# Attention with ALiBi and an MLP on one Trainium2 core: first q and k loaded in FP32 by other queues, the distances of two blocks added on TensorE, and the norm's gain moved into the copies of turned x

## The chip, the cores and the metric

The kernel runs on one core of a Trainium2 chip. The core has five engines that run their own instruction streams in order: TensorE (PE in the profile; PEld is its weight load), VectorE (DVE), ScalarE (ACT), GpSimd (POOL) and SyncE (SP). They wait for one another by semaphores. Transfers are issued by SyncE, ScalarE and GpSimd and run on 16 DMA engines. The metric is device time in microseconds for the whole call, lower is better.

## What is computed

Inputs are `q`, `k`, `v` of 8 batches x 8 heads x 576 tokens x 64, in FP32, and the MLP's gain (512), `w_ch1` (512 x 2048) and `w_ch2` (2048 x 512).

```python
scores = q @ k.T / sqrt(64);  rel = i - j
scores = where((rel >= 0) & (rel < 128), scores - slope[h] * abs(rel), -1e9)   # slope[h] = 2 ** -(h + 1)
attn = softmax(scores);  x = concat_heads(attn @ v)          # (8, 576, 512)
xn = (x - mean(x)) / sqrt(var(x) + 1e-6) * g_ln
out = x + relu(xn @ w_ch1) @ w_ch2
```

Each query sees at most 128 keys: those of its own block of 128 and of the block before.

## The kernel before

**Tiling.** Batches go in pairs; a pair has nine blocks of 128 query rows: two for each of four stretches of 128 tokens (one per batch, so blocks 0 and 1 are tokens 0 to 127 of the two batches and have no block before them, blocks 2 and 3 are tokens 128 to 255), and a ninth for the last 64 tokens of both. Blocks 0 to 7 make four groups of two, all later ones groups of four. Group 0 is blocks 0 and 1, group 1 blocks 2 and 3.

**One block's way.** The raw tokens of q and k are loaded (`load_qk`, L217: by GpSimd, which casts to FP16 on the way), turned on TensorE (`turn`, L323; `turn_first`, L371, for blocks 0 and 1) through PSUM and copied out by VectorE and ScalarE. `attend` (L405) makes scores in PSUM bank pair `ps_sc[0]` or `ps_sc[1]` in turn, and ScalarE takes the exponent. `masks` (L446) multiplies by `m_full`, `m_ends` or `m_tail` on VectorE: tables of exp(-slope x distance), zero outside the window, that `decay` (L145) makes on ScalarE from a table of distances. `values` (L473, in two halves of four heads) or `values_at_once` (L504) multiplies by v with a column of ones beside it, so that the sum of the weights comes along; VectorE takes the reciprocal and writes x with its row sum. `centre` (L535) subtracts the mean. For blocks 0 to 3 it also multiplies by g, spread over all partitions by a matmul with a row of ones (`spread_g`, L301, `g_row`). `turn_x` (L577) turns the block on TensorE and copies it to `xT`.

**The MLP.** `mlp1` (L736) multiplies one group by w1 in 16 units of 128 hidden rows, four matmuls each, with a Relu after each unit on ScalarE, or on VectorE for the units listed in `on_dve`. `mlp2` (L767) multiplies by w2; its result is scaled by the row's 1/std and added to x. Groups 0 and 1 (`FIRST_GROUPS = 2`) are multiplied by w1 itself, which is why their x carries g; later groups use `w1g`, which `gain_w1` (L188) makes on VectorE.

**Order.** The order on each engine is written out by hand: `steps` is a list of lists of calls. The first ones, up to `first`, run before any MLP work; `weave_at` then runs a group's `mlp1` or `mlp2` and, after the units named by its places, takes further steps. A step's instructions enter each engine's stream at that place. `warm(n)` (L294) puts n matmuls of 512 columns, whose result nobody reads, into TensorE's stream. The part up to `first`:

```python
steps = warm_step(11) + [[(turn_first,)]] + warm_step(3)
steps += [scores_step(0), scores_step(1) + masks_of(0) + masks_of(1)] + warm_step(6)
steps += values_steps(0)
steps += [turn_step(2, True, (nc.scalar.copy, nc.scalar.copy))]
steps += values_steps(1) + warm_step(4)
steps += [x_step(0, nc.scalar.copy)] + warm_step(2) + [scores_step(2)]
steps += [masks_of(2, 1) + x_step(1) + scores_step(3), values_steps(2)[0]]
steps += [masks_of(2)]
```

so all scores of blocks 0 to 3 stand before `mlp1(0)`. Loads have an order of their own (`loads`, `place`, `load_until`), all on GpSimd's queue: q and k of blocks 0 and 1, v0, v1, q and k of blocks 2 and 3, v2, v3, four quarters of w1, half of w2, and so on. At most eight of GpSimd's loads are under way: the ninth waits until the first has landed. SyncE loads the distances, an identity matrix and g.

Of the kernel before, what the change touches and what calls it, by code (L numbers as in the profile page):

```python
# [17 lines left out]
P = 128  # L18
# [45 lines left out]
FAR = 60000.0  # L64


def distances():
# [14 lines left out]
    cols = [m[:, evens_first] for m in both] + [*ends, tail]  # L82
    return np.concatenate(cols, axis=1).astype(np.float16)
# [3 lines left out]
def kernel(  # L87
# [41 lines left out]

    iden_dram = nc.inline_tensor(np.eye(P, dtype=np.float16), name="iden16")  # L130
    dist_dram = nc.inline_tensor(distances(), name="distances")
    dist = consts.tile([P, 5 * P], FP16)
    nc.sync.dma_start(out=dist, in_=dist_dram.ap())
    iden = consts.tile([P, P], FP16)
# [4 lines left out]
    nc.sync.dma_start(out=iden, in_=iden_dram.ap())  # L139
# [5 lines left out]
    def decay(m, at):  # L145

        n = m.shape[2]
        for h in range(H):
            nc.scalar.activation(
                out=m[:, h, :],  # L150
                in_=dist[:, at * P : at * P + n],
                func=AF.Exp,
                scale=-(2.0 ** (-8.0 * (h + 1) / H)),
            )

    g_sb = consts.tile([P, NKB], FP32)
    nc.sync.dma_start(out=g_sb, in_=moe_g_ln.rearrange("(kb p) -> p kb", p=P))

    g_line = out_pool.tile([P, DM], FP32, tag="o", name="g_line")[0:1]
    nc.sync.dma_start(out=g_line, in_=moe_g_ln.rearrange("(o d) -> o d", o=1))  # L160
    g_row = out_pool.tile([P, DM], FP32, tag="o", name="g_row")
    one_line = consts.tile([1, P], FP32)
# [15 lines left out]
    ht_all = consts.tile([P, NFB, 4 * P], FP16)  # L178
    w1r = moe_w_ch1.rearrange("(kb p) f -> p kb f", p=P)
# [86 lines left out]
    weights = {3: w1s + w2s[:2], 5: w2s[2:]}  # L266
    loads, place = [], []
    for n, (p, blk) in enumerate(order):
        of_v = [(load_v, p, blk)]
        if n >= V_FIRST:  # L270
            loads += of_v
        if blk % 2 == 0:
# [27 lines left out]

    def spread_g():  # L301

        ps = ps_mm.tile([P, DM], FP32, tag="mm", name="ps_g")
        nc.tensor.matmul(ps, one_line, g_line, start=True, stop=True)
        return ps
# [65 lines left out]
    def turn_first():  # L371

        q, k = queries(0, 0), keys_tile("k", 0, 0)
        ps = [bank(b)[:, 0] for b in range(2)]
        transposed("q", 0, 0, ps)
        for b in range(2):
            nc.vector.tensor_copy(out=q[:, b], in_=ps[b])
        ps_row = spread_g()
        warm(2)
        ps = [bank(b)[:, 0] for b in (0, None)]  # L380
        transposed("k", 0, 0, ps)
        for b, copy in enumerate((nc.scalar.copy, nc.vector.tensor_copy)):
            copy(out=k[:, b].rearrange("p h (c r) -> p r h c", r=2), in_=ps[b])
        nc.vector.tensor_copy(out=g_row, in_=ps_row)
# [19 lines left out]

    def attend(p, blk, keys, mask, tag, hps, sc=None):  # L405
# [15 lines left out]
        ps = banks.rearrange("p j (n t q) -> p j n t q", n=len(hps), t=nk)  # L421
        qt, b = turned["q", p, blk // 2], blk % 2
        for n, hp in enumerate(hps):
            for t, o in enumerate(keys):
                kt = turned["k", p, o // 2][:, o % 2]
                for c, r, queries in seen(p, blk, o, t):
                    cols = slice(c * HALF, (c + 1) * HALF)
                    for j in range(2):
                        rows = slice(j * HALF, (j + 1) * HALF)
                        nc.tensor.matmul(  # L430
                            in_halves(ps[cols, j, n, t, :])[:, r, queries],
                            kt[rows, hp, cols],
                            in_halves(qt[rows, b, hp])[:, r, queries],
                            start=True,
                            stop=True,
                        )
# [7 lines left out]
        unmasked.setdefault((p, blk), []).append((dst, mask[:, heads, :]))  # L444
# [59 lines left out]
    def values_at_once(p, blk):  # L504
# [3 lines left out]
        ps = ps_sc[0].rearrange("p g (h e) -> p (g h) e", h=4)  # L508
# [26 lines left out]
    def centre(p, blk):  # L535
# [3 lines left out]
        if p * NSLOT + blk < BY_DMA:  # L539
# [13 lines left out]
        if p == 0 and blk < FIRST:  # L553
            nc.vector.scalar_tensor_tensor(
                out=xc,
                in0=xs[p, blk],
                scalar=mean,
                in1=g_row,
                op0=ALU.subtract,
                op1=ALU.mult,  # L560
            )
        else:
            nc.vector.tensor_scalar(  # L563
                out=xc, in0=xs[p, blk], scalar1=mean, scalar2=None, op0=ALU.subtract
            )
# [11 lines left out]
    def turn_x(g, at, p, blk, copy):  # L577
# [6 lines left out]
        copy(out=xT[:, :, at * P : (at + 1) * P], in_=ps)  # L584
# [82 lines left out]


    steps = warm_step(11) + [[(turn_first,)]] + warm_step(3)
    steps += [scores_step(0), scores_step(1) + masks_of(0) + masks_of(1)] + warm_step(6)  # L670
    steps += values_steps(0)
    steps += [turn_step(2, True, (nc.scalar.copy, nc.scalar.copy))]
    steps += values_steps(1) + warm_step(4)
    steps += [x_step(0, nc.scalar.copy)] + warm_step(2) + [scores_step(2)]
    steps += [masks_of(2, 1) + x_step(1) + scores_step(3), values_steps(2)[0]]
    steps += [masks_of(2)]
    first = len(steps)

    steps += [values_steps(2)[1] + masks_of(3)]
    steps += [x_step(2, nc.scalar.copy), *values_steps(3), x_step(3, nc.scalar.copy)]  # L680
# [5 lines left out]
    steps += [values_steps(4)[1], scores_step(5) + [(decay, m_ends, 2)]]  # L686
    steps += [x_step(4) + masks_of(5)]
    steps += [values_steps(5)[0], turn_step(6, True), values_steps(5)[1], scores_step(6)]
    steps += [x_step(5) + masks_of(6), scores_step(7) + variance_of(4), values_steps(6)[0]]
# [471 lines left out]
    nc.vector.memset(ones, 1.0)  # L1161
    for vx in vext:
        nc.vector.memset(vx[:, :, D : D + 1], 1.0)
    nc.vector.memset(magic, 0x5F3759DF)
    nc.vector.memset(one_line, 1.0)
    decay(m_full, 0)
    decay(m_tail, 4)
    load_until(place[3])
    engine = mybir.EngineType
    with tc.manual_schedule(engines={engine.PE}):  # L1170
        with tc.manual_schedule(engines={engine.Activation, engine.DVE, engine.SP, engine.Pool}):
            advance_to(first)
            weave_at(mlp1(0, (0, 1)), 2, 7, 8, 9, 13)
# [60 lines left out]
```

## Time and profile before

| | |
|---|---|
| median of 3 runs | 307.45 us (307.02 to 308.31) |
| the profiled execution | 307.49 us, span of the trace 305.7 us |
| TensorE busy | 297.9 us, 97% of the span |
| VectorE, ScalarE, GpSimd busy | 80%, 60%, 37% |
| moved by DMA | 38.03 MB; HBM read 36.90 MB, written 9.44 MB |

Times in the trace count from the start of the span. A line of a timeline gives the start, how long the group of instructions took, engine and source line, output <- inputs, shape, count, and in brackets the idle time before it with what ended it. A line of the table of waits gives who waited for whom: total us, times, the longest.

### The profile page before, as it was taken

To read this page: it belongs to the slowest core of one execution; us is meant where nothing else is said; L and a number is where in the kernel's file an instruction comes from. 1 tells how busy PE (TensorE), PEld (TensorE's weight loads), DVE (VectorE), ACT (ScalarE), POOL (GpSimd) and SP (SyncE) were. 2 spreads that over 40 slices of the span, in tenths; PEclk is the share of its full clock that TensorE was granted. 3 is DMA by queue.
4 is the path that set the end of the run, shared out by engine and by line. 5 is a ranking of instruction groups with operands and counts; after the bars stand their busy time and mean duration, and the time that the engine had idled before them with its cause. 6 is when DMAs were issued, how large, how long until landed. Compare 5 with 4: busy or idle time off the path is not lost.

```text
span 305.7 us, 9273 instructions
## 1 busy us (share of the span) xinstructions
PE 297.9 (97%) x3782; PEld 203.6 (67%) x3782; DVE 245.7 (80%) x651; ACT 182.4 (60%) x329; POOL 111.7 (37%) x152
## 2 busy tenths in 40 slices
PE   8889999999999999999999999999999999999994
PEld 2468755856755578646865686568656865698883
DVE  2689878889986899679867986798799878978993
ACT  7588775767966863675368635853586268505500
POOL 8923659673774372475107250760000000000000
PEclk9999999999999999999999999999999999999999
DMA  9999999999999999999999999997661043005014
GB/s 112 172 206 200 189 158 165 196 131 100 138 120 193 145 132 141 182 182 132 131 172 130 114 131 159 121 154 95 97 130 38 19 102 72 19 19 137 3 34 103
DMA packets 150172, 38.03 MB, mean 124 GB/s; under 512 B 140785, under 2 KB 146033, under 8 KB 150130
## 3 DMA queue, kind: packets, MB, share of 16 engines
q0 software_dynamic: 103744, 18.36, 89.0%
q1 hardware_dynamic: 45906, 18.70, 37.7%
q8 instruction: 29, 0.48, 0.7%
q10 hardware_dynamic: 480, 0.39, 0.5%
q14 instruction: 13, 0.11, 0.1%
HBM read 36.90 MB, written 9.44 MB: 152 GB/s over the span
## 4 chain that ended last, share of the span: by engine, by line
PE 90%; DMA 5%; POOL 2%; ACT 2%; issue 1%; DVE 0%; ACTq 0%; POOLq 0%
PE ps_m L746 36%; PE ps_s L976 25%; PE ps_m L776 9%; PE ps_sc L430 6%; PE ps_sc L512 4%; PE ps_q L1055 4%; PE ps_x L870 3%; DMA q<-q 3%; DMA k<-in_k_dram 2%; PE ps_pv L483 1%; POOL q L223 1%; ACT probs L438 1%; PE ps_tr L317 1%; PE ps_sc L317 1%; POOL vx L258 1%
## 5 line engine op out<-in xcount | busy, mean ns | idle before, releaser
L746 PE MATMUL ps_m<-xT,w1g 128*128 128x512 f16 (+1 forms) x512 | 103.8, 353 | 0.0
L762 ACT ACTIVATE ht_all<-ps_m 128x512 f16<-128x512 f32 (+1 forms) x143 | 71.7, 511 | 26.5 <-PE ps_m L746 24.5
L438 ACT ACTIVATE probs<-ps_sc 128x1024 f16<-128x1024 f32 x56 | 56.5, 1029 | 46.4 <-PE ps_sc L430 46.4
L746 PEld LDWEIGHTS <-w1g 128*128 128x128 f16 x512 | 47.6, 98 | 42.6 <-issue 0.4
L258 POOL DMA_DIRECT2D vx<-in_v_dram x40 | 34.0, 859 | 67.1 <-PE ps_sc L512 38.4
L976 PE MATMUL ps_s<-w,s 128*128 128x256 f16 x384 | 43.8, 273 | 0.0
L976 PEld LDWEIGHTS <-s 128*128 128x128 f16 x384 | 36.7, 98 | 4.7
L449 DVE TENSOR_TENSOR probs<-probs,m 128x1024 f16<-128x1024 f16 x56 | 36.9, 684 | 2.5 <-ACT probs L438 2.5
L976 PE MATMUL ps_s<-w,ht_all 128*128 128x256 f16 x288 | 34.3, 273 | 0.0
L776 PE MATMUL ps_m<-w,ht_all 128*128 128x512 f16 x128 | 31.3, 380 | 0.0
L976 PEld LDWEIGHTS <-ht_all 128*128 128x128 f16 x288 | 27.4, 98 | 5.0
L247 POOL DMA_DIRECT2D q<-in_q_dram x40 | 27.4, 698 | 4.9 <-DMA vx<-in_v_dram 2.9
L997 DVE SCALAR_TENSOR_TENSOR o<-ps_s,rstd,x 128x256 f32<-128x256 f32 x48 | 21.0, 478 | 8.4 <-PE ps_s L976 8.4
L796 DVE TENSOR_TENSOR s<-ht_all 128x1024 f16<-128x1024 f16 (+2 forms) x36 | 20.5, 571 | 7.9 <-ACT ht_all L762 6.7
L430 PE MATMUL ps_sc<-q,k 64*64 64x128 f16 (+1 forms) x1088 | 24.1, 209 | 1.1 <-ACT probs L438 0.7
L430 PEld LDWEIGHTS <-k 64*64 64x64 f16 x1088 | 15.8, 106 | 13.1 <-issue 10.9
L594 ACT ACTIVATE junk<-xc 128x512 f16<-128x512 f16 x28 | 17.6, 628 | 5.7 <-DVE xc L563 5.6
L244 POOL DMA_DIRECT2D k<-in_k_dram x20 | 17.9, 910 | 6.8 <-DMA k<-k 5.3
L521 DVE SCALAR_TENSOR_TENSOR x<-ps_sc,rec 128x512 f16<-128x512 f32 x28 | 19.4, 692 | 1.0
L997 DVE SCALAR_TENSOR_TENSOR o<-ps_s,rstd,o 128x256 f32<-128x256 f32 x36 | 15.7, 478 | 3.4 <-PE ps_s L976 3.1
L776 PEld LDWEIGHTS <-ht_all 128*128 128x128 f16 x128 | 11.1, 98 | 10.8
L512 PEld LDWEIGHTS <-probs 128*128 128x128 f16 x352 | 14.6, 98 | 3.5
(109 smaller groups left out, 381.8 us busy)
## 6 DMA issues: line engine op xcount, KB each, us to landing
out_dram<-o SPq DMA_DIRECT2D x64, 128.0 KB, 2.4
k<-in_k_dram POOLq DMA_DIRECT2D x32, 128.0 KB, 6.9
vx<-in_v_dram POOLq DMA_DIRECT2D x32, 128.0 KB, 8.0
w<-in_moe_w_ch_dram POOLq DMA_DIRECT2D x8, 512.0 KB, 10.9
q<-in_q_dram POOLq DMA_DIRECT2D x48, 64.0 KB, 6.3
q<-in_q_dram POOLq DMA_DIRECT2D x12, 128.0 KB, 5.4
out_dram<-o SPq DMA_DIRECT2D x10, 64.0 KB, 1.9
k<-in_k_dram POOLq DMA_DIRECT2D x8, 64.0 KB, 6.7
```

Of the source, the lines that this page charges most:

```text
L247: nc.gpsimd.dma_start(out=t[half, b], in_=tokens.rearrange("h (c r) d -> r c h d", r=2)[r],)
L258: nc.gpsimd.dma_start(out=vx[p0 : p0 + n, :, 0:D], in_=v[b, :, t0 : t0 + n, :].rearrange("h p d -> p h d"),)
L430: nc.tensor.matmul(in_halves(ps[cols, j, n, t, :])[:, r, queries], kt[rows, hp, cols], in_halves(qt[rows, b, hp])[:, r, queries], start=Tr ...
L438: nc.scalar.activation(out=dst.rearrange("p (n j) q -> p j n q", j=2), in_=ps.rearrange("p j n t q -> p j n (t q)"), func=AF.Exp, scale=in ...
L449: nc.vector.tensor_tensor(out=dst, in0=dst, in1=mask, op=ALU.mult)
L512: nc.tensor.matmul(ps[:, h, 0 : D + 1], pr[:, h, t, :], vext[(p * NSLOT + o) % NV][:, h, :], start=(n == 0), stop=(n == len(terms) - 1),)
L746: nc.tensor.matmul(ps[:, 0:cols], w[:, kb, fb * P : (fb + 1) * P], xT[:, kb, 0:cols], start=(kb == 0), stop=(kb == NKB - 1),)
L762: nc.scalar.activation(out=ht[:, fb, :], in_=ps[:, 0:cols], func=AF.Relu)
L776: nc.tensor.matmul(sums[at], ht[:, fb, at * P : (at + 1) * P], w2[:, fb, :], start=(fb == 0), stop=(fb == NFB - 1),)
L796: nc.vector.tensor_tensor(out=out, in0=a, in1=b, op=op)
L976: nc.tensor.matmul(ps[:, pair, :], lhs[:, fb, at : at + P], rhs[:, fb, :], start=(first and pair == 0 and fb == 0), stop=(fb == half - 1), ...
L997: nc.vector.scalar_tensor_tensor(out=outs[at][:, cols], in0=ps[:, pair], scalar=rstd[:, n : n + 1], in1=(xs[p, blk] if fresh else outs[at] ...
```

## The change

- **First q and k.** The raw tokens of blocks 0 and 1 are no longer loaded by GpSimd with a cast, but in FP32 by SyncE (q) and ScalarE (k), each batch by itself, into parts of the hidden tile `ht_all` that `mlp1` writes later. q stands in partitions 0 to 63, k in 64 to 127. `turn_first` turns them by FP32 matmuls with an FP32 identity, one batch at a time.
- **GpSimd's queue** starts with v0, v1, the first quarter of w1, q and k of blocks 2 and 3, v2, the second quarter, v3, then the rest of w1 and half of w2. The other half of w2 goes one block earlier, and the tables for `m_ends` and `m_tail` follow as a load of their own.
- **Distances on TensorE.** For blocks 0 and 1 VectorE makes eight tables of -slope x distance x 8 (`slopes`), and TensorE writes them into the score banks by a matmul with the identity (`add_distances`); the scores are added on top. Those blocks need no masks. `FAR` falls from 60000 to 16000.
- **g.** `spread_g` and `g_row` are gone; `centre` only subtracts. For groups 0 and 1 `turn_x` multiplies by g in the copy: on VectorE one operation, on ScalarE four.
- **Order.** There are 7 warm matmuls first, not 11. The steps up to `first` hold blocks 0 and 1 alone; the turn, scores and values of blocks 2 and 3 come in `mlp1(0)`, from its unit 3 on. Relus of units 4, 5 and 6 of `mlp1(0)` go to VectorE too. `m_full` is made in three parts, `m_tail` after block 6's scores. Blocks 0 and 1 use `values_at_once`.

```diff
-FAR = 60000.0
+FAR = 16000.0
+ADDED = 2
...
+    def load_first(queue, src, b):
+        rows = slice(0, HALF) if src is q else slice(HALF, P)
+        queue.dma_start(
+            out=first_qk[b][rows],
+            in_=src[b, :, 0:P, :].rearrange("h (c r) d -> c h r d", r=2),
+        )
+    def load_tables():
+        nc.gpsimd.dma_start(out=more_tables, in_=tables_dram[:, 3 * P :])
+    def slopes():
+        for h in range(H):
+            nc.vector.tensor_scalar(
+                out=bias[:, h],
+                in0=first_tables[:, 2 * P :],
+                scalar1=-(2.0 ** (-8.0 * (h + 1) / H)) / inv_sqrt_d,
+                scalar2=None,
+                op0=ALU.mult,
+            )
...
-    weights = {3: w1s + w2s[:2], 5: w2s[2:]}
+    weights = {1: w1s[:1], 2: w1s[1:2], 3: w1s[2:] + w2s[:2], 4: w2s[2:], 5: [(load_tables,)]}
...
+    def turn_first(b, copy):
...
+        for hp in range(HP):
+            for r in range(2):
+                for t, dst in enumerate(ps):
+                    rows = slice(t * HALF, (t + 1) * HALF)
+                    for j in range(2):
+                        cols = slice(j * HALF, (j + 1) * HALF)
+                        nc.tensor.matmul(
+                            dst[cols, r, hp, :],
+                            first_qk[b][rows, 2 * hp + j, r, :],
+                            iden32[rows, rows],
+                            start=True,
+                            stop=True,
+                        )
+        nc.vector.tensor_copy(out=q[:, b], in_=ps[0])
+        copy(out=k[:, b].rearrange("p h (c r) -> p r h c", r=2), in_=ps[1])
...
+    def add_distances(banks):
+        for j in range(2):
+            nc.tensor.matmul(
+                banks[:, j].rearrange("p (n c) -> p n c", n=HP),
+                iden,
+                bias.rearrange("p (n j) c -> p j n c", j=2)[:, j],
+                start=True,
+                stop=False,
+                skip_group_check=True,
+            )
...
-                            start=True,
+                            start=not added,
...
-        if p == 0 and blk < FIRST:
-            nc.vector.scalar_tensor_tensor(
-                out=xc,
-                in0=xs[p, blk],
-                scalar=mean,
-                in1=g_row,
-                op0=ALU.subtract,
-                op1=ALU.mult,
-            )
...
-        copy(out=xT[:, :, at * P : (at + 1) * P], in_=ps)
+        dst = xT[:, :, at * P : (at + 1) * P]
+        if g >= FIRST_GROUPS:
+            copy(out=dst, in_=ps)
+            return
+
+        if copy == nc.vector.tensor_copy:
+            nc.vector.tensor_tensor(
+                out=dst, in0=ps, in1=g_sb.unsqueeze(2).broadcast_to([P, NKB, P]), op=ALU.mult
+            )
+            return
+        for kb in range(NKB):
+            nc.scalar.activation(
+                out=dst[:, kb], in_=ps[:, kb], func=AF.Copy, scale=g_sb[:, kb : kb + 1]
+            )
...
+    (low2, high2), (low3, high3) = ([[(attend, *args)] for args in attends(*order[n])] for n in (2, 3))
+    steps = warm_step(7)
+    steps += [[(slopes,), (nc.vector.tensor_copy, iden32, iden), (decay, m_full, range(3))]]
+    steps += [[(turn_first, 0, nc.scalar.copy)], [(add_distances, ps_sc[0])]]
+    steps += [[(decay, m_full, range(3, 5))]]
+    steps += [[(turn_first, 1, nc.vector.tensor_copy)], [(add_distances, ps_sc[1])]]
+    steps += [scores_step(0), scores_step(1)] + warm_step(3)
+    steps += [[(values_at_once, 0, 0, 0), (centre, 0, 0)]] + warm_step(3)
+    steps += [[(values_at_once, 0, 1, 1)], x_step(0, nc.scalar.copy), [(centre, 0, 1)]] + warm_step(2)
+    steps += [x_step(1)]
     first = len(steps)
+    steps += [[(decay, m_full, range(5, H))] + turn_step(2)] + warm_step(3)
+    steps += [low2, high2 + masks_of(2, 1)] + warm_step(2) + [low3 + masks_of(2)]
+    steps += [values_steps(2)[0], high3 + masks_of(3, 1), values_steps(2)[1]]
+    steps += [values_steps(3)[0], x_step(2), values_steps(3)[1], x_step(3)]
...
+    def start():
+        load_first(nc.sync, q, 0)
+        load_first(nc.scalar, k, 0)
+        nc.sync.dma_start(out=first_tables, in_=tables_dram[:, 0 : 3 * P])
+        load_first(nc.scalar, k, 1)
+        load_first(nc.sync, q, 1)
+        nc.sync.dma_start(out=g_sb, in_=moe_g_ln.rearrange("(kb p) -> p kb", p=P))
+        load_until(place[3])
...
-            weave_at(mlp1(0, (0, 1)), 2, 7, 8, 9, 13)
+            weave_at(mlp1(0, (0, 1, 4, 5, 6)), 3, 3, 3, 3, 3, 3, 4, 5, 6, 7, 8, 9, 11)
```

More of the change, by code (lines that the diff above doesn't have):

```diff
@@ L81, in distances @@
     both = [far(P + query - key), far(query - key)]
-    cols = [m[:, evens_first] for m in both] + [*ends, tail]
+    cols = [np.eye(P), *(m[:, evens_first] for m in both), *ends, tail]
     return np.concatenate(cols, axis=1).astype(np.float16)
@@ L127 @@
     )
[L130 to L134, printed above, removed]
+    tables_dram = nc.inline_tensor(tables(), name="tables").ap()
+    first_tables = consts.tile([P, 3 * P], FP16)
+    more_tables = consts.tile([P, 3 * P], FP16)
+    iden = first_tables[:, 0:P]
+    iden32 = consts.tile([P, P], FP32)
     ps_sc = [
```

93 lines of the change are left out of this document (39 added, 54 removed).

## The prediction

> **What bounds the kernel now.** I read the page first, then the waits of TensorE, then the timelines of TensorE, ScalarE and VectorE over the first 50 us.
>
> ```profile
> PE 90%; DMA 5%; POOL 2%; ACT 2%; issue 1%; DVE 0%; ACTq 0%; POOLq 0%
> ```
> ```profile
> PE ps_warm L299 <- DVE vx L1163: 1.5, 1, 1.5
> PE ps_sc L430 <- ACT probs L438: 0.7, 2, 0.5
> PE ps_sc L317 <- DMA k<-in_k_dram: 0.6, 2, 0.4
> PE ps_tx L583 <- DVE xc L554: 0.3, 1, 0.3
> ```
> The chain that ends last is TensorE. All its waits lie before 19.2 us: asked for the rest of the span, the table of waits shows none. So what counts is when TensorE has done a given amount of useful work; from there the end follows at a fixed distance. The timeline of TensorE gives the marks:
>
> ```profile
> 1.46 4.88 PE L299 MATMUL ps_warm<-ones 128*128 128x512 f16 x11 [1.46 <-DVE vx L1163]
> 6.26 0.44 PE L317 MATMUL ps_sc<-iden,q 64*64 64x64 f16 x32
> 6.64 1.12 PE L304 MATMUL ps_g<-g_line,one_line 1*128 1x512 f32 x2
> 10.07 1.47 PE L299 MATMUL ps_warm<-ones 128*128 128x512 f16 x6
> ...
> 19.16 1.47 PE L746 MATMUL ps_m<-xT,w 128*128 128x256 f16 x12
> ...
> 26.65 8.02 PE L746 MATMUL ps_m<-xT,w 128*128 128x256 f16 x72
> ```
> The 72 are units 14 and 15 of group 0's first product (8 matmuls, 0.11 us each) and the 64 of group 1's. **Mark M**, the first matmul of `mlp1(1)`, is at 26.65 + 0.87 = 27.5 us. By M both kernels have done the same useful work (scores, values and turned x of blocks 0 to 3, all of `mlp1(0)`); behind it TensorE's order is the same. So the change is worth the shift of M, as long as nothing behind it is moved. The difference inside: before, blocks 2 and 3 have their scores done when `mlp1(0)` starts at 19.16; afterwards only blocks 0 and 1 have.
>
> **The change, part by part: the front.** I walk the new order with these rows.
>
> ```profile
> 3.05 2.56 ACT L149 ACTIVATE m<-dist 128x256 f16<-128x256 f16 x8 [1.03 <-DMA dist<-distances]
> 9.97 1.94 ACT L438 ACTIVATE own<-ps_sc 128x1024 f16<-128x1024 f32 x2 [0.52 <-PE ps_sc L430]
> ```
> ```profile
> 9.39 0.67 DVE L384 COPY g_row<-ps_g 128x512 f32<-128x512 f32 x1
> 14.04 0.75 DVE L554 SCALAR_TENSOR_TENSOR xc<-x,mean,g_row 128x512 f16<-128x512 f16 x1
> ...
> 31.27 4.30 DVE L193 TENSOR_SCALAR w1g<-w,g_sb 128x512 f16<-128x512 f16 x13
> ```
> *Tables.* `dist` (160 KB), alone, landed at 3.05. Now q and k of batch 0 (0.52 MB in FP32) share the way with 0.1 MB of tables. The loads of the page's 5 to 10 us wrote 158 GB/s in FP16, so read 316 GB/s; 0.46 MB more is 1.5 us: 4.4 us (ends: 3.05, as `dist`, and 6.0, if q1, k1 and v0 take their part too). Batch 1 lands near 7.
>
> *VectorE before the first turn.* Eight `slopes` and the copy to `iden32` stand before it: nine of 128x128, between 0.08 (a quarter of L193's 0.33) and 0.21 (a 128x1 `mean`); I take 0.14, so 1.3 us. The first turn starts at 5.8.
>
> *FP32 turns.* 32 matmuls of 64 columns per batch. The L304 pair took 1.05 us to the next matmul for 512 columns, so 0.13 us for 64; the FP16 turns ran 32 in 0.28 us, which at 0.027 us each (64 columns at the 0.215 us per 512 of the later warm matmuls) is some 3 side by side. Hence 1.2 us a batch; ends 0.28 (no dearer than FP16) and 4.2 (one after another). The first is at half speed until 6.3 (the first eleven warm matmuls are 0.44 apart, the later ones 0.215): 5.8 to 7.3. `add_distances`, two of 512, 0.44: 7.7. Second turn to 8.9, its distances to 9.3.
>
> *Copies, softmax, values.* An FP32 copy of 512 columns is L384's 0.6 apart. VectorE has q1, k1 from 9.1 to 10.4; scores of block 1 at 10.5, its exponent on ScalarE (0.92 apart) 11.0 to 11.9. The masks of blocks 0 and 1 are gone (0.61 each on VectorE), but three warm matmuls stand before block 0's values: 11.4. Then on VectorE per block: reciprocal 0.25, x 0.73, mean 0.19, centre 0.30 (as later `values_at_once` blocks at 95.2 us ran), 1.47 together: block 0 centred at 13.35, block 1 at 14.8. Its turn, then the multiplication by g from PSUM, 0.64 (between the plain copy's 0.34 and L554's 0.67): 16.0. ScalarE's four pieces of block 0 (0.2 each, as the 128x128 decays) are done before. **`mlp1(0)` starts at 16.1**, 3.1 earlier than before.
>
> *Loads.* GpSimd issues v0, v1 (0.9 each from 1.24), then the first quarter of w1 at 3.0; the longest of the first two quarters' landings before was 10.9 after issue, so by 14 at the latest: hidden. The third, wanted at 25.4, has 3.1 MB in FP16 terms ahead of it and itself, at the 190 GB/s of the page's third to sixth slices 16 us from 2.8: hidden too. q2 and k2 follow at 3.8 to 6.7, landed some 5.8 later, needed at 17.9. g_sb is last on SyncE and needed at 13.9; its cover is 6 us.
>
> **The middle.** Units 0 to 3 run to 17.85 (16 x 0.109), the turn of q2, k2 to 18.4. Then TensorE's order stands at block 2's and 3's scores before unit 4, and ScalarE is late for them: two Relus (to 18.5), three decays (0.95, to 19.4), two copies (0.48, 0.59, to 20.5), then exponents of 0.92: 21.4, 22.35, 23.3. Block 3's low scores need the first PSUM bank back: 21.55. Unit 4 starts at 21.85, where before units 3 to 7 ran through. From here VectorE is the limit: four masks (0.61), three Relus of units 4 to 6 (0.375), four halves of values (0.21 + 0.35 to 0.46), two means and centres (0.25 + 0.30), block 2's g multiplication (0.64), with one gap of 0.3: 8.0 us from 21.55 to 29.6. Before, these three Relus and the copies of x2 and x3 were on ScalarE. TensorE's own work for units 4 to 11 is 3.5, values 1.0, the last scores 0.3, one turn of x 0.2, so it waits some 2.9 in all, in three places: ahead of the values of block 3, the turn of x2, the turn of x3 (at 29.7). Units 12 to 15 then take 1.75: **M at 31.7, 4.2 later than 27.5.**
>
> Removed work that pays nothing of this: `spread_g` and its copy, and centre falling from 0.67 to 0.30, are inside the walk. *The tail's decay* (8 in 1.69) moves to the gap before block 7's exponents:
>
> ```profile
> 53.05 1.94 ACT L438 ACTIVATE probs<-ps_sc 128x1024 f16<-128x1024 f32 x2 [1.56 <-PE ps_sc L430]
> ```
> 1.56 us are free there: 0.1 late, and the Relus behind it run 0.29 apart against 0.437 of TensorE, with four PSUM buffers: nothing; without that cover 1.7. VectorE enters the variances 0.4 later relative to M and had 0.68 idle at 35.6: nothing. `more_tables` lands long before 47 us.
>
> Sum: the profiled execution has 307.49 us (span 305.7), beside a median of 307.45. 307.49 + 4.2 = 311.7.
>
> **The clock, rival A.** TensorE's first matmuls are 0.44 apart from 1.46 until 6.26, then 0.215: 4.8 us of unbroken work before full speed. Now there are seven (3.1 us, to 4.5) and then a pause until 5.8. If the pause makes the 4.8 us count anew, the clock opens at 10.6: the first turn takes 2.4, its distances 0.87, the second turn 1.95, and M is 2.1 later, **313.8**. For: the pause. Against: of the 4.8 us before 6.3, 3.6 are still work. [...]
>
> **Rival B: the middle costs nothing.** One mechanism: if VectorE gets from block 2's first mask to block 3's centre in 5.2 instead of 8.0 us, TensorE never waits behind unit 4 and M is 2.9 earlier: **308.8**, no change that can be told; with the front at its low ends too (first turn at 4.5, 0.28 a batch: `mlp1(0)` at 13.6, -2.5), 306.3, faster. It decides from 6.5 us of VectorE work downwards. Against: between 17.6 and 26.3 of the trace these same instructions stand back to back at these distances.
>
> **Rival C: the loads come late.** Tables at 6.0, batch 1 at 9: first turn 7.4, `mlp1(0)` at 17.5, **313.1**. For: in 5 to 10 us the DMA engines already carried 158 GB/s, and FP32 now writes twice the bytes. Against: SyncE's and ScalarE's issues start at 0.74, GpSimd's at 1.24. [...]
>
> **Rival D: FP32 turns one after another**, 4.2 each: M 6.0 later still, **317.7**. Against: the code alternates halves of rows and columns as the FP16 turns do.
>
> That the change does not do what it says is no rival: each of its pieces is in the order of the engines.
>
> **How the numbers follow.** Forecast 0.52, at 311.7 (its own range 309.6, with FP32 at 0.28 a batch, to 313). A 0.16, C 0.10, D 0.07, B 0.15, of which 0.10 is no change and 0.05 faster. A measurement of this kernel tells some 0.5% (1.5 us) from none. Slower: 0.52 + 0.16 + 0.10 + 0.07 = 0.85. The range from 308.7 to 314.2 leaves out D and the fast part of B.
>
> **What would show it.** First `ps_first` matmul near 5.8 and 1.2 us a batch; `mlp1(0)` from 16.1; TensorE waiting for VectorE's xc and masks between 25 and 30; M near 31.7; no waits of TensorE behind it. M before 29 us would prove the middle wrong, `mlp1(0)` before 14 the front.

## The result and the profile after

The changed kernel takes **316.49 us** (median of 6 runs, 316.14 to 316.78) against 307.88 us for the kernel before (6 runs, 307.02 to 311.45): 1.0263 times, 95% interval 1.0212 to 1.0313. Slower, as forecast, by 8.6 us where 4.2 were forecast. The profiled execution has 316.41 us and a span of 314.6 us, 8.9 more than before. The kernel before ran again beside the experiments, with medians of 307.9 to 308.1. The profiled execution of the last experiment (14) ran at a granted clock of 0.95 and took 315.48 us; neither it nor its trace is used.

The chain that ends last is still TensorE, with more of other engines in it:

```profile
PE 89%; DVE 4%; DMA 2%; ACT 2%; issue 1%; SPq 0%
```

The waits of TensorE (who waited for whom: total us, times, longest) begin with one that was not there before:

```profile
PE ps_first L416 <- DVE iden L792: 5.0, 1, 5.0
PE ps_tx L628 <- DVE xc L608: 2.6, 4, 0.8
...
PE ps_m L808 <- DVE xT L635: 0.9, 1, 0.9
```

The timeline of TensorE gives the marks of the prediction:

```profile
1.52 3.17 PE L334 MATMUL ps_warm<-ones 128*128 128x512 f16 x7 [1.52 <-DVE vx L1235]
9.66 1.99 PE L416 MATMUL ps_first<-iden,ht_all 64*64 64x64 f32 x64 [4.97 <-DVE iden L792]
11.58 1.04 PE L448 MATMUL ps_sc<-ht_all,first_tables 128*128 128x512 f16 x2
12.54 1.89 PE L416 MATMUL ps_first<-iden,ht_all 64*64 64x64 f32 x64
...
21.66 1.91 PE L808 MATMUL ps_m<-xT,w 128*128 128x256 f16 x16 [0.88 <-DVE xT L635]
...
35.14 8.90 PE L808 MATMUL ps_m<-xT,w 128*128 128x256 f16 x80
```

(One FP32 matmul of the program is two records, hence x64.) The first turn stands at 9.66 and not 5.8, `mlp1(0)` at 21.66 and not 16.1. The last line begins with units 12 to 15, 16 matmuls of 0.11, so mark M is 36.9, where 31.7 was forecast and 27.5 was before. The shift of 9.4 is kept: `mlp2(0)` starts at 43.88 against 34.51, and half a microsecond is won back by the end. What held the first turn is seen in the waits of VectorE and in the list of loads (queue, size, median us from issue to landing):

```profile
DVE ht_all L206 <- DMA first_tables<-tables: 6.8, 1, 6.8
```
```profile
ht_all<-in_k_dram ACTq DMA_DIRECT2D x2, 256.0 KB, 5.9
ht_all<-in_q_dram SPq DMA_DIRECT2D x2, 256.0 KB, 7.2
first_tables<-tables SPq DMA_DIRECT2D x1, 96.0 KB, 7.0
```

SyncE issues the tables at 1.54; they land at 8.56, when VectorE can start its nine instructions for the first turn.

### The profile page after: what moved, and what is told of

The parts are those of the page before. It is cut to its first block, busy times and chain, and to the rows that moved or that the text cites. A ratio compares the mean times of both kernels' runs of the same rounds, so it can differ in the third digit from the quotient of the medians.

```text
span 314.6 us, 9389 instructions
## 1 busy us (share of the span) xinstructions
PE 298.9 (95%) x3840; PEld 205.1 (65%) x3840; DVE 245.3 (78%) x657; ACT 179.9 (57%) x325; POOL 109.7 (35%) x149
## 4 chain that ended last, share of the span: by engine, by line
PE 89%; DVE 4%; DMA 2%; ACT 2%; issue 1%; SPq 0%
PE ps_m L808 35%; PE ps_s L1038 24%; PE ps_m L838 9%; PE ps_sc L483 6%; PE ps_sc L567 4%; PE ps_q L1117 4%; PE ps_x L932 3%; DMA first_tables<-tables 2%; PE ps_first L416 1%; PE ps_tx L628 1%; DVE x L576 1%; PE ps_pv L538 1%; ACT own L492 1%; ACT probs L492 1%; DVE x L547 1%
## 5 line engine op out<-in xcount | busy, mean ns | idle before, releaser
L824 ACT ACTIVATE ht_all<-ps_m 128x512 f16<-128x512 f32 (+1 forms) x140 | 70.6, 513 | 31.7 <-PE ps_m L808 29.8
L504 DVE TENSOR_TENSOR probs<-probs,m 128x1024 f16<-128x1024 f16 x56 | 36.9, 683 | 3.7 <-ACT probs L492 3.7
L858 DVE TENSOR_TENSOR s<-ht_all 128x1024 f16<-128x1024 f16 (+2 forms) x36 | 20.5, 570 | 7.9 <-ACT ht_all L824 6.7
L576 DVE SCALAR_TENSOR_TENSOR x<-ps_sc,rec 128x512 f16<-128x512 f32 x30 | 20.7, 691 | 1.0
L838 PEld LDWEIGHTS <-ht_all 128*128 128x128 f16 x128 | 11.1, 98 | 10.8
L492 ACT ACTIVATE own<-ps_sc 128x1024 f16<-128x1024 f32 x12 | 12.2, 1033 | 9.0 <-PE ps_sc L483 9.0
```

The source lines that it names most:

```text
L492: nc.scalar.activation(out=dst.rearrange("p (n j) q -> p j n q", j=2), in_=ps.rearrange("p j n t q -> p j n (t q)"), func=AF.Exp, scale=in ...
L504: nc.vector.tensor_tensor(out=dst, in0=dst, in1=mask, op=ALU.mult)
L576: nc.vector.scalar_tensor_tensor(out=x.rearrange("p (h d) -> p h d", h=H), in0=ps[:, :, 0:D], scalar=1.0, in1=rec.unsqueeze(2).broadcast_t ...
L824: nc.scalar.activation(out=ht[:, fb, :], in_=ps[:, 0:cols], func=AF.Relu)
L838: nc.tensor.matmul(sums[at], ht[:, fb, at * P : (at + 1) * P], w2[:, fb, :], start=(fb == 0), stop=(fb == NFB - 1),)
L858: nc.vector.tensor_tensor(out=out, in0=a, in1=b, op=op)
```

## The experiments

Three theories. **Tables:** they land late because of where they stand among the loads. **Clock:** 7 warm matmuls and a pause of 5.0 us leave TensorE at half clock through both FP32 turns. **Middle:** the scores of blocks 2 and 3 in `mlp1(0)`, and VectorE's queue behind them, cost what was forecast. The marks, in us from the start of the span, are those of each kernel's profiled execution; the last column is the median of all its runs:

| kernel | first turn | second turn | `mlp1(0)` | M | median time |
|---|---|---|---|---|---|
| before | 6.26 (FP16) | | 19.16 | 27.5 | 307.9 |
| forecast | 5.8 | 7.7 | 16.1 | 31.7 | 311.7 |
| after | 9.66 | 12.54 | 21.66 | 36.9 | 316.5 |
| tables first | 6.58 | 9.91 | 18.34 | 35.0 | 314.2 |
| 24 warm | 9.66 | 11.73 | 20.21 | 37.1 | 316.3 |
| both | 8.27 | 10.07 | 18.48 | 33.7 | 314.4 |
| Relus back | 9.47 | 12.36 | 21.81 | 37.7 | 317.0 |
| both, Relus back | 8.15 | 10.29 | 18.70 | 33.4 | 312.9 |
| 24 warm, fillers | 10.37 | 12.27 | 20.76 | 36.0 | 315.3 |
| all repairs | 8.38 | 10.14 | 18.80 | 33.7 | 313.2 |
| scores ahead | 8.02 | 9.93 | 22.22 | 31.8 | 312.9 |
| scores ahead, FP16 loads | 7.42 (FP16) | | 19.15 | 28.8 | 309.9 |

**1. Tables first.**

```diff
     def start():
+        nc.sync.dma_start(out=first_tables, in_=tables_dram[:, 0 : 3 * P])
         load_first(nc.sync, q, 0)
         load_first(nc.scalar, k, 0)
-        nc.sync.dma_start(out=first_tables, in_=tables_dram[:, 0 : 3 * P])
```

The tables go ahead of q of batch 0 on SyncE.

> The load of the first tables (96 KB, the identity and the distances) is moved ahead of q of batch 0 on SyncE; nothing else. Theory 1 (the front is late because the tables stand behind the 512 KB rows of k and q of batch 0): the tables land by 3 to 4.5 us in place of 8.56, VectorE's slopes and iden32 are done before q and k of batch 0 land, and the first turn starts with that landing, at 6.5 to 7.5 in place of 9.66; the kernel is 2 to 3 us faster, about 314. Rival (whatever is on the way to DRAM between 2 and 8 us lands late, in whichever order it is issued): the tables land early, but q of batch 0 then lands at 8 or later, and the gain is under 1 us. The clock, if the pause after the warm matmuls closes it (theory 2), still opens some 4.8 us after the first turn begins, so the turns stay at 1.9 us.

314.24 us (313.61 to 314.94), ratio 1.0192 (1.0157 to 1.0228), so 2.2 us less than the changed kernel. From the list of loads and the timeline of TensorE:

```profile
first_tables<-tables SPq DMA_DIRECT2D x1, 96.0 KB, 2.0
```
```profile
6.58 1.16 PE L416 MATMUL ps_first<-iden,ht_all 64*64 64x64 f32 x64 [1.89 <-DMA ht_all<-in_q_dram]
...
9.91 1.26 PE L416 MATMUL ps_first<-iden,ht_all 64*64 64x64 f32 x64 [1.63 <-DMA ht_all<-in_q_dram]
```

The same load lands 2.0 us after issue in place of 7.0, and the first turn is 3.1 earlier. Two readings go beyond the expectation. Batch 1 lands only at 9.9: the second turn waits for it. And the turns take 1.2 us, not 1.9: in this execution the clock opened between the last warm matmul (4.7) and the first turn, with only 7 warm matmuls. But it fell again; the table of stretches shows it (stretch, its length, busy us of TensorE, of its weight load, VectorE, ScalarE and GpSimd, each with the count, then granted clock, DMA share, GB/s):

```profile
19.00:22.00 3.00, 3.00 (x56) 2.03 (x58) 0.82 (x2) 0.86 (x3) 1.36 (x2) 0.50 1.35 203
```

Granted clock 0.50 from 19 to 22: units 0 to 3 of `mlp1(0)` take 3.14 in place of 1.91. That is why M gained 1.9 where the first turn gained 3.1 and `mlp1(0)` 3.3.

**2. 24 warm matmuls** (`warm_step(24)` for `warm_step(7)`).

> 24 warm matmuls ahead of the first turn in place of 7; nothing else. Theory 2 (the pause from 4.7 to 9.66 keeps the granted clock at half until 14.25): the clock opens near 6.3 as in the kernel before, the warm matmuls end near 9.3, the two turns take 0.95 to 1.0 us each in place of 1.9, their distances 0.45 to 0.5 in place of 1.0, and the kernel is 1.7 to 2.3 us faster, about 314.5. Rival (the FP32 turns are dear by themselves, whatever the clock, and the exponents and copies behind them set the pace): turns stay at 1.9, gain under 0.5 us.

316.26 us (314.99 to 316.63), ratio 1.025 (1.0212 to 1.0288): no gain that can be told.

```profile
9.66 1.16 PE L416 MATMUL ps_first<-iden,ht_all 64*64 64x64 f32 x64 [0.50 <-DVE iden L792]
...
20.21 3.38 PE L808 MATMUL ps_m<-xT,w 128*128 128x256 f16 x16 [0.88 <-DVE xT L635]
```

The turns did what the clock theory said, 1.2 us each, and `mlp1(0)` started 1.45 earlier. Then its first 16 matmuls took 3.38 in place of 1.91 and gave all of it back. The stretches of this run:

```profile
16.00:19.00 3.00, 1.55 (x17) 0.79 (x16) 2.67 (x10) 1.05 (x4) 1.50 (x3) 1.00 1.48 194
19.00:22.00 3.00, 2.12 (x13) 1.39 (x14) 1.12 (x2) 0.10 (x1) 1.43 (x3) 0.64 1.55 194
22.00:25.00 3.00, 3.00 (x80) 1.80 (x78) 1.12 (x3) 1.76 (x6) 1.05 (x2) 0.79 1.24 208
```

TensorE is busy for 1.55 of the 3 us from 16 to 19; then half clock follows, 2 x 0.36 x 3 + 2 x 0.21 x 3 = 3.4 us of it. Whether that is the cause is the question of run 11.

**3. Both** (tables first, 18 warm).

> Both at once: the tables first on SyncE, and 18 warm matmuls in place of 7. Theory 1 and 2 together: first turn near 7 at full clock, mlp1 of group 0 from 17 to 17.5 in place of 21.66, and the kernel 4 to 5 us faster, about 312, which is the forecast's own time for a front without the two delays; what is left against the kernel before (some 4 us) is then the middle. Rival (the middle is limited by something that does not move with the front, as the landing of w1 or of the later q and k): mlp1 of group 0 starts early, but the first matmul of mlp1 of group 1 stays within 2 us of 36.9.

314.42 us (313.21 to 315.32), ratio 1.0207 (1.0164 to 1.025). In the profiled execution (313.21) the clock stayed open:

```profile
8.27 1.16 PE L416 MATMUL ps_first<-iden,ht_all 64*64 64x64 f32 x64
...
10.07 1.26 PE L416 MATMUL ps_first<-iden,ht_all 64*64 64x64 f32 x64
...
18.48 1.91 PE L808 MATMUL ps_m<-xT,w 128*128 128x256 f16 x16 [0.87 <-DVE xT L635]
...
31.95 8.90 PE L808 MATMUL ps_m<-xT,w 128*128 128x256 f16 x80
```

M moved with the front, by 3.2 for 3.2, against the rival. The gain is 3 us in such an execution, not 4 to 5, because the second turn now stands behind batch 1's landing; two of the four runs had the half clock (mean clock 0.992) and took 315.0 and 315.3.

**4. Relus back** (`mlp1(0, (0, 1))` for `mlp1(0, (0, 1, 4, 5, 6))`).

> The Relus of units 4 to 6 of mlp1 of group 0 go back from VectorE to ScalarE; nothing else. Theory 3 (from unit 4 to the turn of x3 VectorE's 8 us of work set the pace): VectorE is relieved of 3 x 0.375 us, x3 is turned 0.8 to 1.1 us earlier, and the kernel is 0.5 to 1.1 us faster, about 315.5. Rival (ScalarE's late exponents set the pace, and VectorE merely waits for them): the Relus stand behind the exponents of blocks 2 and 3 on ScalarE, units 4 to 6 free their PSUM banks later, and the kernel is the same or up to 1 us slower.

317.03 us (315.12 to 317.38), ratio 1.0269 (1.0226 to 1.0313). The median says nothing: three of four runs had a mean granted clock of 0.983 or 0.984 and took 317.0 to 317.4; the one at 1.0 took 315.12, 1.4 less than the changed kernel. In the trace `mlp1(0)` to M is 15.9 us, with half clock from 22.2 to 25.6, which costs some 1.7 by an estimate (half of its 3.4 us; in run 2 the 16 matmuls took 3.38 in place of 1.91); without it some 14.2, against 15.2. (The same trace has half clock from 8.5 to 15.3 too; the last section comes back to it.) Inconclusive by itself, hence run 5.

**5. Both, Relus back.**

> The kernel with the tables first and 18 warm matmuls, and the Relus of units 4 to 6 back on ScalarE. Theory 3 (VectorE's queue sets the pace from unit 4 to the turn of x3): the turn of x3 comes 0.8 to 1.2 us earlier, and the kernel is faster by as much, 312.5 to 313. In the run with the Relus alone the same 1 us was gained in this stretch, and hidden by a stretch of half clock. Rival (ScalarE binds once it has them): the mark moves by under 0.3 us.

312.86 us (312.41 to 314.03), ratio 1.0158 (1.0096 to 1.0219). From `mlp1(0)` to M 14.7 us in place of 15.2; TensorE's wait ahead of the turn of x2 fell from 0.60 to 0.17, that ahead of x3 stayed at 0.62. So VectorE's queue binds in this stretch, but three Relus are worth some 0.5 us of it, about half of what was expected.

**6. Loads held, and 7. all loads held**, both on the kernel of run 3, for the landings alone. A GpSimd copy that reads batch 1's tokens is put ahead of GpSimd's loads (in run 7 without the first added line, so that v0 and v1 wait too):

```diff
-        load_until(place[3])
+        load_until(place[1])
+        held = small.tile([P, 1], FP32, tag="held", name="held")
+        nc.gpsimd.tensor_copy(out=held, in_=first_qk[1][:, 0, 0, 0:1])
+        load_until(place[3])
```

> On the kernel with the tables first and 18 warm matmuls, GpSimd holds every load behind v0 and v1 (the first quarter of w1, q2, k2, v2 and the rest) until batch 1 of q and k has landed; nothing else. It is a look at the landings alone, and its time is not read as a gain. Theory 1 (the loads of the front share one stream of some 180 to 200 GB/s, so batch 1, landed at 9.9, stood beside w1, q2 and k2): batch 1 lands 1 to 2 us earlier, at 8 to 9. Rival (SyncE's and ScalarE's loads are paced by their own issue and rows, 512 rows of 512 bytes each, not by what GpSimd has in flight): batch 1 still lands at 9.5 to 10, and the forecast's 7 could not have been had by any order of GpSimd's loads.

> The kernel with the tables first and 18 warm matmuls, and GpSimd holds all of its loads, v0 and v1 too, until batch 1 of q and k has landed. A look at the landings of 1 MB of FP32 rows with nothing else on the way. If v0 and v1 slowed them, batch 1 lands at 7 to 8.5 in place of 10.0; if SyncE's and ScalarE's rows have a pace of their own, at 9.3 to 10 still, and no order of loads gives the forecast's 7.

The copy's line on GpSimd gives the landing, first of run 6, then of run 7:

```profile
10.02 0.18 POOL L1232 COPY held<-ht_all 128x1 f32<-128x1 f32 x1 [6.87 <-DMA ht_all<-in_q_dram]
```
```profile
8.61 0.18 POOL L1231 COPY held<-ht_all 128x1 f32<-128x1 f32 x1 [8.16 <-DMA ht_all<-in_q_dram]
```

Without w1, q2, k2 and v2 on the way batch 1 lands at 10.0, as with them; without v0 and v1 as well, at 8.6. So v0 and v1, issued at 1.24, cost 1.4 us, and with nothing else but 96 KB of tables under way the 1 MB of FP32 rows still needs until 8.6: the forecast's 7 was not to be had by reordering GpSimd's loads. (Times: 314.17 and 313.54, one execution each.)

**8. Tables on ScalarE's queue**, one line of the changed kernel (`nc.scalar.dma_start` for `nc.sync.dma_start`).

> The changed kernel with one line moved to another queue: the first tables are issued by ScalarE, between k of batch 0 and k of batch 1, in place of SyncE. A look at the landings. Reading 1 (a load waits for the rows ahead of it on its own issuer's queue: k of batch 0, landed at 4.8, against q of batch 0, landed at 6.5): the tables land at 5.5 to 6.5 in place of 8.56. Reading 2 (the loads of both engines are worked off in one order, that of their issue, whoever issues): they land at 7.5 to 8.6 still. Reading 3 (96 KB in 128 rows is slow among the other loads wherever it stands): 8.5 or later.

```profile
first_tables<-tables ACTq DMA_DIRECT2D x1, 96.0 KB, 5.0
```

Landed at 6.6: nearest to the first reading, that the tables wait for the rows ahead of them on their own queue. Behind k of batch 0 (landed at 4.6) they landed 2.0 us earlier than behind q of batch 0 in the changed kernel (landed at 6.5); each time it was about 2 us after the load ahead of them. Issued at 1.51 and at 1.54, the same load landed 2 us apart on the two queues. The first turn moved up by 1.7; the time did not (316.47, one run), as the granted clock was one half from 20.5 to 23.9 in it.

**9. Scores ahead**, on the kernel of run 3: q2 and k2 first on GpSimd's queue, and the middle in the order of the kernel before.

```diff
-    steps += [scores_step(0), scores_step(1)] + warm_step(3)
+    steps += [scores_step(0), scores_step(1), turn_step(2)]
...
+    steps += [high2 + masks_of(2, 1), low3, x_step(1)]
     first = len(steps)
...
-            weave_at(mlp1(0, (0, 1, 4, 5, 6)), 3, 3, 3, 3, 3, 3, 4, 5, 6, 7, 8, 9, 11)
+            weave_at(mlp1(0, (0, 1)), 1, 2, 4, 5, 6, 8, 11)
```

> The kernel with the tables first and 18 warm matmuls, and the middle undone: q2 and k2 are loaded ahead of v0, and the turn of q2, k2 and the low and high scores of block 2 and the low scores of block 3 stand ahead of mlp1 of group 0, as they did in the kernel before; Relus of units 4 to 6 and the copy of x2 are on ScalarE. Theory 3 (the later scores of blocks 2 and 3 and VectorE's queue behind them cost the 7 us by which the stretch from mlp1 of group 0 to mlp1 of group 1 grew): that stretch shrinks from 15.2 to 9 to 11 us, the first matmul of mlp1 of group 1 comes at 28 to 30 in place of 33.7, and the kernel is 4 to 5.5 us faster than the one with both edits, about 309. Rival (the stretch is paced by the landing of w1, which is behind 1 MB of FP32): units 8 to 15 wait for w1, the mark stays after 31, and the gain is under 2.5 us.

312.86 us (311.41 to 315.12), ratio 1.0159 (1.0085 to 1.0232).

```profile
16.07 0.38 PE L347 MATMUL ps_tr<-first_tables,k 64*64 64x64 f16 x24 [2.79 <-issue]
...
22.22 1.03 PE L806 MATMUL ps_m<-xT,w 128*128 128x256 f16 x8 [0.88 <-ACT probs L493]
...
30.08 8.90 PE L806 MATMUL ps_m<-xT,w 128*128 128x256 f16 x80
```

From `mlp1(0)` to M it is 9.6 us in place of 15.2: the stretch shrank as the theory said, and units 8 to 15 waited for no w1. The start of `mlp1(0)` moved the other way, 3.7 later, and only in part because more work now stands ahead of it. In the middle of the turn of k2 TensorE was idle for 2.8 us, until 16.07, and the profile shows nothing that it waited for ("issue"): k2's two loads, issued at 2.71 and 3.42, had landed some 8 us later, by 11.4. Half clock from 16.9 to 20.3 followed. So M came at 31.8 and not at 28 to 30, and the kernel gained 1.6 us by the medians and not 4 to 5.5. What TensorE stood still for is open.

**10. The same with FP16 loads.** q and k of batches 0 and 1 come from GpSimd with a cast again and are turned in FP16, with 11 warm matmuls; distances on TensorE and g in the copies stay.

> The same order as the kernel with the scores ahead, but q and k of batches 0 and 1 are loaded by GpSimd in FP16 and turned in FP16, as in the kernel before; the distances are still added on TensorE, g still goes into the copies of turned x, the tables are SyncE's first load, with 11 warm matmuls. Theory 1 (FP32 writes 0.5 MB more into a stream that is full at some 200 GB/s, and v0, v1 wait for nothing else): q and k land at 6 to 9 as in the kernel before, mlp1 of group 0 starts at 16 to 18, its mark is at 26 to 28, and the kernel is the same as the one before or up to 1.5 us faster, 306 to 308.5. Rival (the FP32 loads by SyncE and ScalarE are worth their bytes because GpSimd's issue is the bottleneck): the kernel is slower than the one with the scores ahead.

309.90 us (309.1 to 311.31, 10 runs), ratio 1.0056 (1.003 to 1.0082).

```profile
19.15 1.03 PE L791 MATMUL ps_m<-xT,w 128*128 128x256 f16 x8 [0.88 <-DVE xT L622]
...
27.01 8.90 PE L791 MATMUL ps_m<-xT,w 128*128 128x256 f16 x80
```

`mlp1(0)` starts 3.1 earlier than in run 9, and the kernel is 3.0 us faster. How much of this the FP32 loads are worth is not shown: run 9's trace has the unexplained 2.8 us, and the turns and the warm matmuls changed too. The kernel stays 1.7 slower than the kernel before, and its 309.90 lies 1.4 above the expected range. Half clock from 13.6 to 17.0 is in its trace as well, and g is still in the copies (run 13).

**11. 24 warm matmuls and fillers, and 12. all repairs.** Eight more warm matmuls go into the gaps ahead of `mlp1(0)`; run 11 has the 24 of run 2, run 12 the edits of run 5.

```diff
-    steps += [[(values_at_once, 0, 1, 1)], x_step(0, nc.scalar.copy), [(centre, 0, 1)]] + warm_step(2)
-    steps += [x_step(1)]
+    steps += [[(values_at_once, 0, 1, 1)]] + warm_step(3)
+    steps += [x_step(0, nc.scalar.copy), [(centre, 0, 1)]] + warm_step(4)
+    steps += [x_step(1)] + warm_step(3)
```

> The kernel with 24 warm matmuls, and eight more warm matmuls in the gaps ahead of mlp1 of group 0, where TensorE waits for VectorE: three ahead of the turn of x0, two more ahead of the turn of x1, three behind it. Nothing else. Theory 2 (24 warm matmuls do open the clock in time and save 1.5 us by mlp1 of group 0; a later stretch of half clock, behind a front in which TensorE is busy for less than half of the time, takes it back): no half clock behind 7 us, the sixteen matmuls from the start of mlp1 take 1.9 us in place of 3.4, the mark is at 35.3 to 35.7 in place of 37.1, and the kernel is at 314.5 to 315.2. Rival (the half clock comes from elsewhere, as heat or another stage, and fillers only add work): the same 316 as with 24 warm matmuls alone, with half clock still in the trace.

> The changed kernel with every cheap repair at once: the tables first, 18 warm matmuls, Relus of units 4 to 6 back on ScalarE, and the same eight fillers. Theory: with the clock held, the mark is at 33.0 to 33.5 in all of its executions, and the time 312.3 to 313, with less scatter than without the fillers (312.41 to 314.03). What then stands between it and the kernel before, 4.5 to 5 us, is the middle and batch 1's landing at 10. Rival: the fillers delay the turns of x0 and x1, and the kernel is at 313.5 or later.

Run 11: 315.34 us (314.94 to 315.56), ratio 1.0222 (1.0186 to 1.0258). The same stretch as in run 2, and the start of `mlp1(0)`:

```profile
16.00:19.00 3.00, 2.86 (x31) 1.41 (x28) 2.38 (x9) 0.99 (x4) 1.55 (x3) 1.00 1.58 196
19.00:22.00 3.00, 2.53 (x21) 1.57 (x20) 1.71 (x4) 0.56 (x3) 1.69 (x3) 1.00 1.57 192
```
```profile
20.76 1.91 PE L809 MATMUL ps_m<-xT,w 128*128 128x256 f16 x16 [0.23 <-DVE xT L635]
```

TensorE busy for 2.86 of 3 us, granted clock 1.00, no half clock behind 7 us in the trace (mean clock 0.998 to 1.0 in all six runs, 0.992 in the profiled execution of run 2), and the gain that run 2 had lost is there: 1.15 us under the changed kernel, although its tables landed some 0.7 later, so that the first turn stood at 10.37. (M, at 36.0, and the time lie 0.3 and 0.1 above the ranges expected.) From the first turn to `mlp1(0)` it is 10.4 us in place of 12.0: that 1.6 is the price of the clock in the front.

Run 12: 313.22 us (313.0 to 313.47), ratio 1.0156 (1.012 to 1.0191). The runs lie within 0.5 us, those of run 5 within 1.6. But its M (33.7) is not better than without fillers, and the median lies just above the range expected. So every cheap repair together wins 3.3 of the 8.6 us; 5.3 stay.

**13. One part alone: g in the copies**, on the kernel before. `spread_g`, `g_row` and their load go, `centre` only subtracts, `turn_x` is the changed one.

> One part of the change alone, on the kernel before: g goes into the copies of turned x (four scaled pieces on ScalarE for blocks 0, 2 and 3, one multiplication on VectorE for block 1), the row of g, its spreading over the partitions and its load are gone, and centre only subtracts the mean. By the prediction's rows: VectorE saves the copy of the row and 0.35 per centre of four, ScalarE pays some 0.6 more per block of three; mlp1 of group 0 starts 0 to 0.8 us earlier, and nothing behind it changes: 306.8 to 308. Rival: ScalarE's pieces delay the exponents of blocks 2 and 3 and x3 is turned later, up to 1 us slower.

310.22 us (307.84 to 311.05, 12 runs), ratio 1.0055 (1.0028 to 1.0082): the rival, and dearer than it said. In TensorE's waits stands

```profile
PE ps_sc L418 <- ACT probs L426: 1.7, 2, 1.2
```

where the kernel before had 0.7 (0.5 the longest). The scores of block 3 wait for ScalarE, whose exponents are late: its four pieces of block 0 take 1.17 us where the plain copy took 0.62, and the exponents start at 17.03 in place of 16.50. `mlp1(0)` starts at 20.09 in place of 19.16, so 0.5 of the 0.9 is ScalarE's; half clock from 18.8 to 22.3 lies across that start. The loss is 1.7 us by the ratio. The four executions with a mean clock of 0.998 or more have a median of 308.9, the other eight 310.6: a large part of it comes with the half clock.

**14. A version to beat both:** run 10 with the values of blocks 0 and 1 ahead of the turn of q2, k2, whose two batches are turned apart, and fillers.

```diff
+    steps += [scores_step(0), scores_step(1)] + warm_step(6)
+    steps += [[(values_at_once, 0, 0, 0), (centre, 0, 0)]] + warm_step(2)
+    steps += [[(values_at_once, 0, 1, 1)], [(turn_half, 0, nc.scalar.copy)]]
+    steps += [x_step(0, nc.scalar.copy), [(centre, 0, 1)]] + warm_step(2)
+    steps += [low2] + warm_step(2) + [x_step(1), high2, [(turn_half, 1, nc.vector.tensor_copy)]]
```

> From the kernel with q and k in FP16 and the scores ahead (mark at 28.8, 309.1 at best): block 0's and 1's values stand ahead of the turn of q2, k2, whose two batches are turned apart, so that VectorE takes block 0 at 12.4 in place of 14.5; warm matmuls fill TensorE's gaps from 8.8 to 16, so that no stretch of half clock follows. Theory (the start of mlp1 of group 0 carries the rest with it): it starts at 16.5 to 17.5 in place of 19.15, the mark is at 26 to 27.5, no clock of one half behind 8 us, and the kernel is 0 to 1.5 us faster than the one before, 306.4 to 308. Rival (the landing of w1 or ScalarE's exponents bind as soon as the start is earlier): the mark stays at 27.5 to 28.5, and the kernel is the same as the one before or up to 1 us slower.

308.24 us (median of 11 runs), ratio 1.0004 (0.9982 to 1.0026): the same as the kernel before. That is 0.24 above the expected range, and the time that its rival gave; without a trace the marks are not known. No version was found that beats the kernel before.

## Why the prediction was right or wrong

Direction right, size 4.4 us short, and outside the range. The front was to win 3.1 us by `mlp1(0)` and lost 2.5, wrong in sign; the direction rested on the middle, which cost 6.9 where 7.2 were forecast. M came at 36.9 and not 31.7. Of the 5.2 between, 3.9 are the late first turn (the tables) and 1.7 the half clock (1.0 between the two turns, 0.7 behind the second), less 0.4 of the middle. A third wrong step, batch 1, lay hidden behind these.

- **Tables: wrong, the step that failed first.** 4.4 (ends 3.05 and 6.0) was worked out from bytes, as if all loads under way shared one rate. They landed at 8.56. Run 1 shows that the same 96 KB took 2.0 us ahead of q's rows, and run 8 that the queue it stood in mattered: 5.0 behind k's rows on ScalarE's queue, 7.0 behind q's on SyncE's, each time landed some 2 us after the rows ahead. The end of 6.0, which rival C took too, came from the same wrong picture.
- **Batch 1 near 7: wrong, and hidden behind the tables.** It landed at 11.1 in the changed kernel, where the second turn (12.54) did not wait for it; it lands at 9.9 to 10.0 once the tables are early (runs 1, 3, 6), 8.6 with nothing of GpSimd's beside it (run 7). So of the second turn's 4.8 of lateness run 3 removed 2.4, the tables' and the half clock's together, and the other 2.4 are then batch 1's.
- **Clock, rival A (0.16): it held.** First turn 1.99 and second 1.89 in the profiled execution; the same instructions took 1.16 and 1.26 at full clock (runs 2, 3). Run 11 puts the price at 1.6 us. The rivals were priced as if only one could hold; A and C held together, C with the tables later still than its 6.0 (the shifts of 2.1 and 1.4 add up to 315.2), and the late tables made the pause longer. The reason given for A, the pause, is only half of it. With the same 7 warm matmuls the first turn ran at full clock in run 1 (1.16 at 6.58, a pause of 1.9 us). In run 4 the granted clock fell to one half at 8.5, in the pause, and was back at 1.00 at 15.3; in the changed kernel's trace the matmuls kept half speed until 14.2 (last section). So with a pause of 5 us the turns of both were at half clock; what made the traces differ ahead of that is not shown.
- **VectorE before the first turn: right.** 1.3 us forecast, 1.1 from the landing to the first turn (8.56 to 9.66).
- **FP32 turns: right.** 1.2 us a batch forecast; 1.1 from one turn to its distances at full clock (run 3, 8.27 to 9.36). Rival D was wrong.
- **Copies, softmax, values: right.** Second turn to `mlp1(0)` 8.4 forecast; 8.4 in run 3, 9.1 in the changed kernel with its second turn at half clock.
- **The middle: right, 15.6 forecast, 15.2 measured, and shown.** Put back into the order of before it takes 9.6 (run 9), and rival B fell. In the changed kernel VectorE goes from block 2's first mask to the end of block 3's centre with one gap of 0.22:

```profile
26.93 0.69 DVE L504 TENSOR_TENSOR probs<-probs,m 128x1024 f16<-128x1024 f16 x1 [1.58 <-ACT probs L492]
...
34.50 0.35 DVE L608 TENSOR_SCALAR xc<-x,mean 128x512 f16<-128x512 f16 x1
```

That is 7.9 us where 8.0 were forecast. At the three places named TensorE waited less, 0.26, 0.60 and 0.62 in place of some 2.9 in all. With three Relus off VectorE the stretch shrank by 0.5 and not by 1.1 (run 5), so VectorE is not its only limit.
- **"g ... inside the walk":** its place was right, its price was not tried in the changed kernel. Alone it costs 1.7 us (run 13), which the prediction did not expect. The distances on TensorE were not tried alone.
- **Nothing behind M: right.** 9.4 at M, 8.9 at the end; one wait of 0.2 is new there.

So with the clock kept and the tables early, M would be 31.7 + 2.4 (batch 1) - 0.4 (middle) = 33.7, which is what run 3 has.

## What to carry to other kernels

Where a small table gates the first instruction, issue it first on its queue, ahead of any load of many rows (here 2.0 us to landing and not 7.0); bytes over bandwidth did not tell when it landed (4.4 worked out, 8.56 measured). An early start on TensorE can be returned later: with 24 warm matmuls `mlp1(0)` started 1.45 us earlier, and half clock took all of it back (run 2). With fillers in the gaps as well that did not come (mean clock 0.998 to 1.0 in all eleven executions of runs 11 and 12). When rivals lie in the same stretch and one makes the other likelier, add them up for the range and do not let only one of them hold.

## What the runs showed of the hardware

- A load of 96 KB on SyncE's queue landed 2.0 us after its issue at the head of the queue (run 1) and 7.0 behind 256 KB in 512-byte rows (the changed kernel); on ScalarE's queue, behind the same amount, 5.0 (run 8).
- Four FP32 loads of 256 KB by SyncE and ScalarE, issued from 0.73 to 2.0, were in at 8.6 with only the tables beside them (run 7), at 10.0 with two loads of v (run 6).
- The half clock of the start was seen only in the durations: the granted clock in the tables of stretches reads 1.00 up to a trace's first change, also from 1.5 to 6 us of the kernel before, where the warm matmuls are 0.44 us apart and later ones 0.215. With 7 warm matmuls from 1.52 to 4.69 each time, the first turn took 1.16 at 6.58 in run 1; in the changed kernel it took 1.99 at 9.66, and half speed lasted until 14.2. In run 4 the granted clock fell to one half at 8.5, 3.8 us after the last warm matmul, and was at 1.00 again from 15.3. Why the three differ is not shown.
- Half clock came back without a long pause: in run 2, after 3 us in which TensorE was busy for 1.55 and no gap was over 0.9 us, the granted clock was one half for 3.4 us. With 2.86 of 3 us busy it stayed at 1.00 (run 11). But busy time alone does not tell the two apart: ahead of the half clock from 18.8 in run 1, from 22.2 in run 4 and from 18.8 in run 13 TensorE was busy for 1.53, 1.41 and 1.27 of some 3 us (16 to 19, 19 to 22, 16 to 19), and after 1.53 of 3 us the granted clock stayed at 1.00 in runs 3, 5, 6 and 7 (16 to 19) and in the changed kernel (19 to 22).
